# Pooled attention, then a routed mixture of experts: keys pooled by adding DMAs, no padding rows, a bf16 scale, shorter routing pieces at the end of attention

## Chip, cores, metric

The kernel runs on one core of one Trainium2 chip. The metric is the device time of one execution in microseconds (us). Three runs of the kernel before took 1842.59, 1843.52 and 1837.3 us; the median is 1842.59 us. The profiled execution took 1847.69 us, of which the trace spans 1845.2 us.

## The reference

Shapes: four batches, 12288 query rows each (384 x 32), 128 channels; 768 pooled keys per batch; 8 experts with 1024 hidden units.

```
kv_pool = kv.reshape(B, H//4, 4, W//4, 4, C).mean(axis=(2, 4))
k = v   = kv_pool.reshape(B, -1, C) @ w_sr
x       = softmax(q @ k^T / sqrt(C)) @ v          # 49152 rows of 128
active  = (x @ w_skip) > 0                         # about half of the rows
e_idx   = argmax(x @ w_gate);  gate = softmax(x @ w_gate)[e_idx]
out     = x;   out[active] += gate * (relu(x @ w1[e_idx]) @ w2[e_idx])
```

## The kernel before

**Attention.** The 49152 query rows are 384 tiles of 128, 96 per batch. The instructions of every engine are in the order in which the loop over `t` issues them. In round `t` PE computes the scores of tile `t` (L595 to L597), the weighted sum of tile `t - 6` (`attend`, L658) and transposes of tile `t - 1` (L633); DVE takes the row maximum (L603) and low halves in fp16 (L616, L641), ACT the exponential (L608) and high halves (L612, L640), POOL low halves of q (L577). SP transposes probabilities by DMA (L620).

**Keys.** While batch `b` runs, `load_kv` fetches the keys of batch `b + 1`: for each of 6 chunks, four DMAs from SP of 256 KB, one about every 3.25 tiles, each into a part of its own of the tile `kvt`. `pool_kv` then adds 16 values to one on POOL: seven additions of 128x256 (L437) and one of 128x128 (L440) for a chunk, one in a tile. `with_max` lets each wait for the low half L616, so that it runs beside the row maximum. Batch 0 is pooled in another way ahead of the loop. At tile 84 of a batch the projections for the next one begin (`prep_kv`).

**Routing.** Every 12 tiles (a round `r` of 32) `route` finds expert and place of each row and POOL writes the rows, one indirect DMA for a tile (L183 by L792), to a scratch tensor `scr`, where each expert has a region that is filled upward. Per-expert totals are carried from round to round in `run`, by a matmul (L766). Round 31 alone is cut into three pieces of 4 tiles, whose small operations run on DVE (`few`); rounds up to 30 use 12 tiles and POOL.

**Experts.** Groups of 2048 rows are read back from the upper end of each region; a last group reaches below the region's begin, where 2048 padding rows per expert (32 DMAs of 264 KB, `write_pads`) hold a row number that no write accepts. A group is four sub-steps of 512 rows: `up` (24 matmuls), `down` (24 matmuls), and in the next sub-step `finish`: 4 transposes, 4 scaled additions on DVE (L292) and 4 indirect DMAs into the output. `x_transpose` splits a sub-step's rows in fp16 halves (L247, L255) and transposes them by DMA (L258). `w_scale` finds a power of two for each weight matrix; the maximum over partitions is an fp32 matmul with ones (L197).

**Between the two.** The first group is chosen early (`snapshot`, round 27), its rows are loaded by `first_step`, and its steps (`peel`) are interleaved with the end of attention, two in a round from round 384 on. `make_table` lists all other groups; `flush` then loads the next group. A barrier follows, and the loop over 17 groups (L1006).

**Queues.** Each engine runs its instructions in order. SP issues all DMAs but the indirect ones, so a wait in front of one holds all behind it. POOL issues the indirect ones.

Of the kernel before, what the change touches and what calls it, by code (L numbers as in the profile page):

```python
# [20 lines left out]
RT = 12  # L21
# [3 lines left out]
def kernel(  # L25
# [28 lines left out]
    K1, K2 = 3, 2  # L54
# [24 lines left out]
    BIG = 1 << 20  # L79
    NG = -(-NT // G) + E  # L80
# [4 lines left out]
    scr = dram.tile([E * CAP, ROW], F32, name="scr")  # L85
# [43 lines left out]
    e0 = consts.tile([1, E], F32, name="e0")  # L129
# [3 lines left out]
    def iconst(name, shape, pattern, base):  # L133
        ti = consts.tile(shape, I32, name=name + "_i")
        nc.gpsimd.iota(ti, pattern=pattern, base=base, channel_multiplier=0)
        tf = consts.tile(shape, F32, name=name)
        nc.gpsimd.tensor_copy(tf, ti)
        return tf

    kg = iconst("kg", [1, KMAX], [[G, KMAX]], 0)  # L140
    gi = iconst("gi", [1, NG + 1], [[1, NG + 1]], 0)
    lo_i = iconst("lo_i", [1, E, E], [[1, E], [-1, E]], 0)
# [11 lines left out]
    w_dg = wp.tile([P, 2, P], F32, name="w_dg")  # L154
# [6 lines left out]
    h = {}  # L161

    def alloc_h(pool):
        h.update(hi=pool.tile([P, FC, ST], F16, name="h_hi"), lo=pool.tile([P, FC, ST], F16, name="h_lo"))

    op = ctx.enter_context(tc.tile_pool(name="op", bufs=2))
    tb_p = ctx.enter_context(tc.tile_pool(name="tb_p", bufs=1))
    tabi = tb_p.tile([1, 2 * (NG + 1)], I32, name="tabi")
    cumi = tb_p.tile([1, 1], I32, name="cumi")

    writes, first_writes, finished, ready, loaded, moved = [], [], [], [], [], []
# [19 lines left out]
    def w_scale():  # L191
        for i, w in enumerate((w1_raw, w2_raw.rearrange("p k c -> p (k c)"))):
            nc.vector.tensor_reduce(out=w_max[:, i:i + 1], in_=w, axis=AX.X, op=ALU.max, apply_absolute_value=True)
            nc.vector.tensor_scalar(out=w_dg[:, i, :], in0=ident, scalar1=w_max[:, i:i + 1], scalar2=None, op0=ALU.mult)
# [4 lines left out]
        nc.vector.tensor_scalar(out=w_max, in0=w_max, scalar1=2.0 ** -80, scalar2=None, op0=ALU.max)  # L199
        em = emask.broadcast_to([P, 2])  # L200
        nc.vector.tensor_tensor(out=w_exp[:, 2:4], in0=w_max.bitcast(I32), in1=em, op=ALU.bitwise_and)
        nc.vector.tensor_tensor(out=w_exp[:, 0:2], in0=w_exp[:, 2:4], in1=em, op=ALU.bitwise_xor)
        wf = w_exp.bitcast(F32)
        for i, p in enumerate((WEXP - 1, W2EXP - 1)):
            nc.vector.tensor_scalar(out=w_sc[:, i:i + 1], in0=wf[:, i:i + 1], scalar1=2.0 ** p, scalar2=None,
                                    op0=ALU.mult)
# [29 lines left out]
    def load_start(gidx):  # L236
        return nc.sync.value_load(tabi[0:1, bass.ds(gidx + (NG + 1), 1)], min_val=0, max_val=E * CAP - G)

# [6 lines left out]
    def x_transpose(s, pool=False):  # L245
        for t in range(TT):
            nc.scalar.activation(out=x16[:, 0, t, :], in_=xin[s][:, t, 0:C], func=AF.Copy,  # L247
                                 scale=xin[s][:, t, C + 2:C + 3])
        if pool:
# [3 lines left out]
            nc.gpsimd.tensor_tensor(out=x16[:, 1, :, :], in0=x, in1=x16[:, 0, :, :], op=ALU.subtract)  # L253
        for t in () if pool else range(TT):
            nc.vector.scalar_tensor_tensor(out=x16[:, 1, t, :], in0=xin[s][:, t, 0:C],  # L255
                                           scalar=xin[s][:, t, C + 2:C + 3], in1=x16[:, 0, t, :],
                                           op0=ALU.mult, op1=ALU.subtract)
        nc.sync.dma_start_transpose(xT[s], x16.rearrange("p a t c -> p (a t c)"))  # L258
# [27 lines left out]
    def finish(s):  # L286
        ps = alloc["x"]()
        for t in range(TT):
            nc.tensor.transpose(ps[:, t * P:(t + 1) * P], yTs[s % 2][:, t * P:(t + 1) * P], ident)  # L289
        o = op.tile([P, TT, C], F32, name="o")  # L290
# [4 lines left out]
        for t in range(TT):  # L295
            scatter_rows(out, xin[s].bitcast(I32)[:, t, C + 1:C + 2], o[:, t, :], NT - 1, "out")

    def make_table():
        en = ends[0:1, :]
        cnt = tb_p.tile([1, E], F32, name="cnt")  # L300
        nc.vector.tensor_tensor(out=cnt, in0=en, in1=base0[0:1, :], op=ALU.subtract)
        cmp = tb_p.tile([1, E, KMAX], F32, name="cmp")
        nc.vector.tensor_tensor(out=cmp, in0=cnt.unsqueeze(2).broadcast_to([1, E, KMAX]),
                                in1=kg.unsqueeze(1).broadcast_to([1, E, KMAX]), op=ALU.is_gt)
        yield
        ng = tb_p.tile([1, E], F32, name="ng")
        nc.vector.tensor_reduce(out=ng, in_=cmp, axis=AX.X, op=ALU.add)
        nc.vector.tensor_tensor(out=ng, in0=ng, in1=e0, op=ALU.subtract)
        nc.vector.tensor_tensor(out=lo_i, in0=lo_i, in1=ng.unsqueeze(1).broadcast_to([1, E, E]), op=ALU.mult)
        cum = tb_p.tile([1, E], F32, name="cum")  # L310
        nc.vector.tensor_reduce(out=cum, in_=lo_i, axis=AX.X, op=ALU.add)
        nc.vector.tensor_scalar(out=cumi, in0=cum[:, E - 1:E], scalar1=1.0, scalar2=None, op0=ALU.max)
        yield
        av = tb_p.tile([1, E], F32, name="av")
# [4 lines left out]
        S3 = [1, NG + 1, E]  # L319
        ge = tb_p.tile([1, NG + 1, E + 1], F32, name="ge")  # L320
# [3 lines left out]
        tab = tb_p.tile([1, 2, NG + 1], F32, name="tab")  # L324
        nc.vector.tensor_reduce(out=tab[:, 0, :], in_=ge[:, :, 1:E + 1], axis=AX.X, op=ALU.add)
        nc.vector.tensor_scalar(out=tab[:, 0, :], in0=tab[:, 0, :], scalar1=float(E - 1), scalar2=None, op0=ALU.min)
        yield
        sel = tb_p.tile(S3, F32, name="sel")
        nc.vector.tensor_tensor(out=sel, in0=ge[:, :, 0:E], in1=ge[:, :, 1:E + 1], op=ALU.subtract)
        nc.vector.tensor_tensor(out=sel, in0=sel, in1=av.unsqueeze(1).broadcast_to(S3), op=ALU.mult)  # L330
        nc.vector.tensor_reduce(out=tab[:, 1, :], in_=sel, axis=AX.X, op=ALU.add)
# [3 lines left out]
        nc.vector.tensor_scalar(out=tab[:, 1, :], in0=tab[:, 1, :], scalar1=0.0, scalar2=None, op0=ALU.max)  # L335
        nc.vector.tensor_copy(tabi, tab.rearrange("p a g -> p (a g)"))

    def peel():
        for s in range(NST):
            for c in range(FC):  # L340
# [10 lines left out]
                if s == NST - 1 and c in (1, 3):  # L351
                    scale = w_scale() if c == 1 else scale
                    next(scale, None)
                yield
            if s == NST - 1:
                split_w1()
            for i, _ in enumerate(down(s)):
                if s == NST - 1 and i == 1:
                    x_transpose(1)
# [5 lines left out]
    with ExitStack() as p1:  # L365
# [25 lines left out]
        PK = 4 if TPB >= 64 else 8  # L391
# [3 lines left out]

        PADS = [(e, i) for e in range(E) for i in range(0, G // P, PK)]

        def write_pads(e, i):
            dst = scr[e * CAP + i * P:e * CAP + (i + PK) * P, :].rearrange("(p k) c -> p k c", p=P)
# [6 lines left out]
        def load_kv(b, k, rs=range(R)):  # L406
# [3 lines left out]
            for r in rs:  # L410
                nc.sync.dma_start(KVT[b, k][:, r, :], src[r])
# [151 lines left out]
        LASTR = NTILE // RT - 1  # L563
        SNAPR = LASTR - 4

# [80 lines left out]
        def attend(t):  # L646
# [23 lines left out]
            def scale():  # L670
# [6 lines left out]
                if r >= LASTR:  # L677
# [8 lines left out]
        def route(r, a, b, last, eng):  # L686
# [41 lines left out]
            if not few:  # L728
                for _ in range(3 if r < LASTR - 1 else K1):
# [9 lines left out]
            for _ in range(1 if few else 2 if r < LASTR - 1 else K2):  # L739
                yield  # L740
            yield (None if r >= LASTR - 1 else GT - 1)
            while accs.get("done", 0) != r * RT + a:
                yield (None if r >= LASTR - 1 else GT - 1)
# [18 lines left out]
            else:  # L762
                wa = E * RTP
                ohf = oha.rearrange("p e t -> p (e t)")
                nc.tensor.matmul(ps[:, 0:wa], ones_bf, ohf, start=True, stop=False)
                nc.tensor.matmul(ps[:, 0:wa].rearrange("p (e t) -> p e t", t=RTP)[:, :, 0], ones_f[0:1, :], run[0:1, :],  # L766
                                 start=False, stop=True)
                nc.tensor.matmul(ps[:, wa:2 * wa], upper_bf, ohf, start=True, stop=True)
                pre = rt.tile([P, E, RTP], F32, name="pre")
                accs["run"] = pre[:, :, RT]  # L770
# [293 lines left out]
```

## Time and profile before

| | us |
|---|---|
| median of three runs | 1842.59 |
| profiled execution | 1847.69 |
| its span in the trace | 1845.2 |
| PE busy in the span | 1757.6 |
| DVE, ACT, POOL busy | 1549.4, 1325.3, 1104.0 |

In 40 slices of 46.13 us, busy share in tenths and granted TensorE clock in tenths, the engines stand so:

```profile
PE   4999999999999999999998879999999999999997
...
DVE  7899889999899898898999768878877888778875
...
POOL 2369887889968998766767543333333333333333
PEclk9999999999999999999999989999999999999998
```

Attention is the first 22 slices, the passage to the experts the next two, the loop the rest. PE is the fullest row nearly everywhere, so the reader looks for slices in which it is not, and for what PE itself could be spared where it is.

### The profile page before, as it was taken

The numbers are of one execution on the slowest core, as the hardware profiler recorded it, in microseconds if no ns is written. First come the engines' busy times: TensorE is split into PE (matmuls) and PEld (weight loads), VectorE is DVE, ScalarE is ACT, GpSimd is POOL, SyncE is SP. The second block draws the span as 40 slices with busy tenths as digits, with TensorE's granted clock in tenths as the row PEclk, the third lists the DMA queues.
The fourth block names the chain that finished last, engine by engine and source line by source line (L and its number), as shares of the span: only waits on it lengthen the run. The fifth ranks groups of instructions, "written<-read, shape, count | busy, mean of one in ns | idle before, by whom it ended". The sixth has DMA issues, their size and how long they took to land. (4 is left out here: it accounts for less than half of the span.)

```text
span 1845.2 us, 42946 instructions
## 1 busy us (share of the span) xinstructions
PE 1757.6 (95%) x14017; PEld 1263.0 (68%) x14017; DVE 1549.4 (84%) x3226; ACT 1325.3 (72%) x2518; POOL 1104.0 (60%) x1339
## 2 busy tenths in 40 slices
PE   4999999999999999999998879999999999999997
PEld 3998889888899888899998434444444444444443
DVE  7899889999899898898999768878877888778875
ACT  2888778888888887788887446666666666666664
POOL 2369887889968998766767543333333333333333
PEclk9999999999999999999999989999999999999998
DMA  6999999999999999999999443333333333333342
GB/s 178 192 202 218 220 185 208 220 184 189 178 177 197 206 214 204 200 215 216 228 211 195 92 119 98 95 99 96 93 95 95 102 93 94 94 97 97 98 112 71
DMA packets 621971, 284.88 MB, mean 154 GB/s; under 512 B 503168, under 2 KB 571904, under 8 KB 621824
## 3 DMA queue, kind: packets, MB, share of 16 engines
q1 hardware_dynamic: 600320, 244.56, 66.1%
q0 software_dynamic: 21504, 38.43, 7.0%
q8 instruction: 83, 1.36, 0.3%
q14 instruction: 64, 0.52, 0.1%
HBM read 90.60 MB, written 78.64 MB: 92 GB/s over the span
## 5 line engine op out<-in xcount | busy, mean ns | idle before, releaser
L183 POOL DMA_INDIRECT out_dram<-o,xin x288 | 294.4, 1022 | 481.9 <-DVE o L292 415.4
L183 POOL DMA_INDIRECT scr<-rows,di x384 | 410.6, 1069 | 120.8 <-issue 98.6
L269 DVE SCALAR_TENSOR_TENSOR h_lo<-h_ps,h_hi 128x512 f16<-128x512 f32 x544 | 343.9, 684 | 145.5 <-ACT h_hi L268 145.5
L608 ACT ACTIVATE p_sb<-s_ps,nm 128x768 f32<-128x768 f32 x384 | 347.4, 905 | 142.7 <-DVE nm L603 140.7
L603 DVE TENSOR_REDUCE nm<-s_ps 128x1 f32<-128x768 f32 x384 | 363.6, 947 | 54.4 <-PE s_ps L597 53.5
L268 ACT ACTIVATE h_hi<-h_ps 128x512 f16<-128x512 f32 x544 | 318.5, 597 | 51.6 <-PE h_ps L267 32.1
L658 PE MATMUL acc_ps<-v_hi,pt 128*128 128x138 f16 x3072 | 321.4, 224 | 16.9 <-DVE rs L666 16.5
L658 PEld LDWEIGHTS <-pt 128*128 128x128 f16 x4608 | 276.8, 98 | 82.7 <-issue 81.8
L616 DVE SCALAR_TENSOR_TENSOR p<-p_sb,p 128x512 f16<-128x512 f32 x384 | 298.1, 776 | 4.2 <-ACT p L612 3.6
L595 PE MATMUL s_ps<-k_hi,q_hi 128*128 128x384 f32 x768 | 294.7, 384 | 0.0
L658 PE MATMUL acc_ps<-v_lo,pt 128*128 128x138 f16 x1536 | 294.4, 223 | 0.0
L596 PE MATMUL s_ps<-k_lo,q_hi 128*128 128x384 f32 x768 | 260.4, 339 | 0.0
L597 PE MATMUL s_ps<-k_hi,q_lo 128*128 128x384 f32 x768 | 259.5, 338 | 0.0
L612 ACT ACTIVATE p<-p_sb 128x512 f16<-128x512 f32 x384 | 243.3, 634 | 11.1 <-DMA pt<-p 8.0
L265 PE MATMUL h_ps<-xT,w_hi 128*128 128x512 f16 x544 | 206.9, 380 | 7.7 <-issue 7.7
L266 PE MATMUL h_ps<-xT,w_hi 128*128 128x512 f16 x544 | 206.9, 380 | 0.0
L267 PE MATMUL h_ps<-xT,w_lo 128*128 128x512 f16 x544 | 206.8, 380 | 0.0
L281 PE MATMUL y_ps<-h_hi,w_hi 128*128 128x512 f16 x544 | 206.2, 379 | 0.0
L281 PE MATMUL y_ps<-h_hi,w_lo 128*128 128x512 f16 x544 | 206.2, 379 | 0.0
L281 PEld LDWEIGHTS <-w_hi 128*128 128x128 f16 x1152 | 112.7, 98 | 132.4 <-issue 0.4
L284 ACT ACTIVATE yT<-y_ps,y_sc 128x512 f32<-128x512 f32 x68 | 46.8, 688 | 216.2 <-PE y_ps L281 216.2
L281 PE MATMUL y_ps<-h_lo,w_hi 128*128 128x512 f16 x544 | 195.1, 379 | 0.0
(216 smaller groups left out, 3208.1 us busy)
## 6 DMA issues: line engine op xcount, KB each, us to landing
kvt<-in_kv_dram SPq DMA_DIRECT2D x96, 256.0 KB
q_sb<-in_q_dram SPq DMA_DIRECT2D x96, 256.0 KB
out_dram<-rows SPq DMA_DIRECT2D x96, 256.0 KB
xin<-scr SPq DMA_DIRECT2D x75, 264.0 KB, 2.9
w_raw<-in_moe_w_dram SPq DMA_DIRECT2D x38, 512.0 KB, 4.3
scr<-pad SPq DMA_DIRECT2D x32, 264.0 KB
pt<-p SPq DMA_TRANSPOSE x384
scr<-rows,di POOLq DMA_INDIRECT x384
```

Of the source, the lines that this page charges most:

```text
L183: ins = nc.gpsimd.indirect_dma_start(out=dst, out_offset=bass.IndirectOffsetOnAxis(ap=ids, axis=0), in_=src, in_offset=None, bounds_check= ...
L268: nc.scalar.activation(out=h["hi"][:, c, :], in_=ps, func=AF.Relu)
L269: nc.vector.scalar_tensor_tensor(out=h["lo"][:, c, :], in0=ps, scalar=0.0, in1=h["hi"][:, c, :], op0=ALU.max, op1=ALU.subtract)
L281: nc.tensor.matmul(ps, w[:, c, :], h[x][:, c, :], start=(i == 0), stop=(i == len(terms) - 1))
L595: nc.tensor.matmul(s[:, h, :HK], q_hi, k_hi[:, sl], start=True, stop=False)
L596: nc.tensor.matmul(s[:, h, :HK], q_hi, k_lo[:, sl], start=False, stop=False)
L597: nc.tensor.matmul(s[:, h, :HK], q_lo, k_hi[:, sl], start=False, stop=True)
L603: nc.vector.tensor_reduce(out=NM[t], in_=S_PS[t][:, :, :HK], axis=AX.XY, op=ALU.max, negate=True)
L608: nc.scalar.activation(out=P_SB[t], in_=S_PS.pop(t)[:, :, :HK], func=AF.Exp, bias=NM.pop(t))
L612: nc.scalar.activation(out=P16[t][:, 0, :], in_=p_flat(t)[:, 0:KD * P], func=AF.Copy, scale=2.0 ** PEXP)
L616: LO[:] = [nc.vector.scalar_tensor_tensor(out=p16[:, 1, :], in0=p_flat(t)[:, 0:KD * P], scalar=2.0 ** PEXP, in1=p16[:, 0, :], op0=ALU.mult ...
L658: nc.tensor.matmul(ps[:, j % 2, :], w, v[a][:, k, :], start=(i == 0), stop=(i == len(AVL) - 1))
```

## The change

Keys of batches 1 to 3: SP loads the first of four parts; three DMAs from POOL add the others to it in place. One addition of 128x256 and the last of 128x128 stay on POOL. Padding rows of the experts go; one dummy region of 2048 rows at the end of `scr` stays (4 DMAs). Instead `make_table` works out how far a group reaches below its region (`low`), and `finish` writes row numbers into a tile of its own (`own`), raised where a row lies below. `w_scale` cuts the row maxima to powers of two first and multiplies in bf16. Rounds 30 and 31 are routed in pieces of 4 tiles. Loads of the first group wait only for scatters up to round 27. In the last batch, totals are added on POOL instead of by L766. `x_transpose` has two buffers; output writes of the first group are held back behind the last scatters (`held`); the next group's first two loads come ahead of the transposes of its rows; from round 390 on one step of the first group goes in a round.

```
 def load_kv(b, k, rs=range(R)):
     for r in rs:
-        nc.sync.dma_start(KVT[b, k][:, r, :], src[r])
+        if b == 0 or r == 0:
+            nc.sync.dma_start(KVT[b, k][:, r, :], src[r])
+        else:
+            nc.gpsimd.dma_start(KVT[b, k][:, 0, :], src[r], accum_op=ALU.add)
 def pool_kv(b, k):
-    n = R * R * C
+    n = R * R * C if b == 0 else R * C
-PADS = [(e, i) for e in range(E) for i in range(0, G // P, PK)]
+PADS = list(range(0, G // P, PK))
 def w_scale():
+    nc.vector.tensor_tensor(out=w_max.bitcast(I32), in0=w_max.bitcast(I32), in1=emask..., op=ALU.bitwise_and)
-    nc.tensor.matmul(ps[:, 0:2 * P], ones_f, w_dg.rearrange("p a x -> p (a x)"), start=True, stop=True)
+    nc.tensor.matmul(ps[:, 0:2 * P], ones_bf, w_dg.rearrange("p a x -> p (a x)"), start=True, stop=True)
 def finish(s, g=None):
+    nc.vector.scalar_tensor_tensor(out=own, in0=place[:, s, :].unsqueeze(2), scalar=low[:, bass.ds(g, 1)],
+                                   in1=ids, op0=ALU.add, op1=ALU.max)
+    if g is None and not ready: held.append(write)
+    else: write()
 def peel():
-    if s == NST - 1 and c in (1, 3): ... next(scale, None)
-    if s == NST - 1: split_w1()
+    if s == NST - 1 and c == 6: x_transpose(1)
+    scale = w_scale() if s == NST - 1 else ()          # first half behind the last up
     for i, _ in enumerate(down(s)):
-        if s == NST - 1 and i == 1: x_transpose(1)
+        if s == NST - 1 and i == 1: next(scale, None); split_w1()
-                if r >= LASTR:
+                if r >= FEWR:                          # LASTR - 1
 def route(...):
+    totals = r * RT < NTILE - TPB
+    if not totals: eng.tensor_tensor(out=accs["run"], in0=run, in1=pre[:, :, RT], op=ALU.add)
+                   eng.tensor_tensor(out=acc, in0=acc, in1=em(run), op=ALU.add)
 def load_rows(st, s, after, group=None):
+    tc.declare_no_dep(ins, group="scr", keep=after, reason="rows read first are complete")
-            while finished and (finished[0] == 0 or len(moved) > 1):
+            while finished and (finished[0] <= 1 or len(moved) > 1):
-            for _ in range(2 * (t >= NTILE)): next(first)
+            for _ in range(0 if t < NTILE else 2 if t < NTILE + LAG else 1): next(first)
```

On POOL, while batch 0 runs, a stretch of the order before (`q_lo` is the low half of q, `kvt` the key tile, `pooled` its sum, `oh_all` a routing tile):

```order
L437 TENSOR_TENSOR kvt<-kvt 128x256
L183 DMA scr<-rows,di 409600x132
L437 TENSOR_TENSOR kvt<-kvt 128x256
L183 DMA scr<-rows,di 409600x132
L577 TENSOR_TENSOR q_lo<-q_sb,q_hi 128x256
L437 TENSOR_TENSOR kvt<-kvt 128x256
L183 DMA scr<-rows,di 409600x132
L440 TENSOR_TENSOR pooled<-kvt 128x128
```

and the same place now:

```order
L188 DMA scr<-rows,di 411648x132
L443 DMA kvt<-in_kv_dram 128x1x512
L188 DMA scr<-rows,di 411648x132
L610 TENSOR_TENSOR q_lo<-q_sb,q_hi 128x256
L188 DMA scr<-rows,di 411648x132 x2
L771 TENSOR_TENSOR oh_all_94<-oh,act 128x12x8
L610 TENSOR_TENSOR q_lo<-q_sb,q_hi 128x256
L443 DMA kvt<-in_kv_dram 128x1x512
```

Additions on POOL have become DMAs that POOL issues, in among the scatters.

On POOL from the scatters of round 29 to the barrier in front of the loop, before (`di` are places, `xin` rows read back, `o` results):

```order
L789 IOTA rows 128x12
L183 DMA scr<-rows,di 409600x132 x12
L789 IOTA rows 128x4
L183 DMA scr<-rows,di 409600x132 x4
L789 IOTA rows 128x4
L183 DMA scr<-rows,di 409600x132 x4
L183 DMA out_dram<-o,xin_134 49152x128 x4
L789 IOTA rows 128x4
L183 DMA scr<-rows,di 409600x132 x4
L183 DMA out_dram<-o,xin_135 49152x128 x4
L183 DMA out_dram<-o,xin_136 49152x128 x4
L993 TENSOR_LOAD cumi
```

and now:

```order
L827 IOTA rows 128x12
L188 DMA scr<-rows,di 411648x132 x2
L827 IOTA rows 128x4
L188 DMA scr<-rows,di 411648x132 x6
L827 IOTA rows 128x4
L188 DMA scr<-rows,di 411648x132 x12
L827 IOTA rows 128x4
L188 DMA scr<-rows,di 411648x132 x4
L827 IOTA rows 128x4
L188 DMA scr<-rows,di 411648x132 x4
L827 IOTA rows 128x4
```

The first piece before begins with round 30 (round 29 stands ahead of it); now round 29's twelve stand in among the first two pieces of round 30, four pieces follow (the last two have the same two rows again), and all twelve output writes come after the last scatter.

On SP, the loads of the next group (`xin_134` is the first 512 rows, `xT_142` and `xT_139` are the transposed rows of the first group's last sub-step and of the next group's first), before:

```order
L258 DMA_TRANSPOSE xT_142<-x_138 128x8x128
L224 TENSOR_LOAD tabi
L224 ISA x2
L231 ISA
L231 DMA w_raw<-in_moe_w_dram 128x1024
L234 ISA
L234 DMA w_raw<-in_moe_w_dram 128x8x128
L237 TENSOR_LOAD tabi
L237 ISA x2
L189 ISA
L189 DMA xin_134<-scr 128x528
L258 DMA_TRANSPOSE xT_139<-x_138 128x8x128
```

and now (`xin_139`, `xT_147`, `xT_144` are the same three):

```order
L240 DMA w_raw<-in_moe_w_dram 128x8x128
L243 TENSOR_LOAD tabi
L243 ISA x2
L194 ISA
L194 DMA xin_139<-scr 128x528
L264 DMA_TRANSPOSE xT_147<-x16b 128x8x128
L194 ISA
L194 DMA xin_140<-scr 128x528
L264 DMA_TRANSPOSE xT_144<-x_143 128x8x128
```

The load, which waits for the last scatter, now stands ahead of the transpose that the first group's last sub-step needs.

## Rows read from the trace of the kernel before

**Rows 1.** Stretch, length; busy PE, PEld, DVE, ACT, POOL (count); PEclk, DMA share, GB/s.

```profile
311.00:492.00 181.00, 175.20 (x1887) 161.21 (x1885) 165.39 (x312) 149.39 (x280) 161.57 (x202) 1.00 1.05 195
804.50:950.00 145.50, 144.46 (x1568) 133.40 (x1565) 130.52 (x268) 123.00 (x233) 99.15 (x131) 1.00 1.12 221
...
1100.00:1800.00 700.00, 700.00 (x3372) 336.65 (x3371) 557.62 (x1250) 451.53 (x866) 263.71 (x258) 1.00 0.37 97
```

**Rows 2.** The row maximum, once a tile: stretches of batches 0, 1, 2, 3.

```profile
L603 DVE TENSOR_REDUCE nm<-s_ps x72: 887/950/959, 64.6 to 244.2; 128x1 f32<-128x768 f32 x72
...
L603 DVE TENSOR_REDUCE nm<-s_ps x72: 889/950/958, 311.1 to 490.3; 128x1 f32<-128x768 f32 x72
...
L603 DVE TENSOR_REDUCE nm<-s_ps x61: 893/950/959, 557.3 to 710.6; 128x1 f32<-128x768 f32 x61
...
L603 DVE TENSOR_REDUCE nm<-s_ps x60: 893/950/959, 804.7 to 949.0; 128x1 f32<-128x768 f32 x60
```

**Rows 3.** Groups with shapes, batch 1 (311 to 492 us).

```profile
L183 POOL DMA_INDIRECT scr<-rows,di x71 | 77.8, 1096 | 15.2 <-issue 11.5 <-POOL rows L789 2.5 <-DVE nm L603 0.5
...
L616 DVE SCALAR_TENSOR_TENSOR p<-p_sb,p 128x512 f16<-128x512 f32 x72 | 57.3, 796 | 0.7 <-ACT p L612 0.7
...
L437 POOL TENSOR_TENSOR kvt<-kvt 128x256 f32<-128x256 f32 x38 | 32.9, 865 | 0.5
```

**Rows 4.** The same groups, batch 3 (804.5 to 950 us).

```profile
L183 POOL DMA_INDIRECT scr<-rows,di x59 | 61.9, 1049 | 26.7 <-issue 25.4 <-POOL rows L789 0.7 <-DVE ptq L641 0.3
...
L616 DVE SCALAR_TENSOR_TENSOR p<-p_sb,p 128x512 f16<-128x512 f32 x60 | 43.7, 728 | 2.1 <-ACT p L612 2.1
```

**Rows 5.** PE, timeline, in the loop: start us, us, instruction.

```profile
1160.83 0.59 PE L197 MATMUL x_ps<-w_dg,ones_f 128*128 128x256 f32 x2
1161.26 0.38 PE L281 MATMUL y_ps<-h_hi,w_hi 128*128 128x512 f16 x1
1161.48 0.38 PE L281 MATMUL y_ps<-h_hi,w_lo 128*128 128x512 f16 x1
```

**Rows 6.** PE, timeline, end of attention; in brackets the idle before.

```profile
1012.02 0.29 PE L658 MATMUL acc_ps<-v_hi,pt 128*128 128x138 f16 x2
...
1013.11 0.38 PE L633 MATMUL acc_ps<-ident,p_sb 128*128 128x128 f32 x2
...
1019.53 0.38 PE L766 MATMUL misc<-pre,ones_f 1*128 1x8 f32 x2
1019.85 0.22 PE L768 MATMUL misc<-oh_all,upper_bf 128*128 128x104 bf16 x1
...
1026.15 0.19 PE L754 MATMUL misc<-oh_few,upper_bf 128*128 128x40 bf16 x1 [3.70 <-DVE acc L775]
...
1070.43 0.67 PE L197 MATMUL misc<-w_dg,ones_f 128*128 128x256 f32 x2 [3.10 <-DVE w_dg L194]
...
1088.22 0.58 PE L265 MATMUL h_ps<-xT,w_hi 128*128 128x512 f16 x1 [7.67 <-issue]
```

**Rows 7.** POOL, timeline, the same stretch.

```profile
1003.64 1.09 POOL L183 DMA_INDIRECT scr<-rows,di  x1 [1.60 <-issue]
...
1034.63 1.05 POOL L183 DMA_INDIRECT scr<-rows,di  x1 [7.84 <-DVE di L788]
1035.99 0.98 POOL L183 DMA_INDIRECT scr<-rows,di  x1 [0.30 <-issue]
...
1080.26 1.08 POOL L183 DMA_INDIRECT out_dram<-o,xin  x1 [0.30 <-issue]
```

**Rows 8.** SP's DMA queue, timeline, the same stretch.

```profile
1072.54 0.35 SPq L189 DMA_DIRECT2D xin<-scr  x1
...
1083.67 1.24 SPq L258 DMA_TRANSPOSE xT<-x  x1
```

**Rows 9.** DMA issues: count, KB each, median us to landing.

```profile
xin<-scr SPq DMA_DIRECT2D x75, 264.0 KB, 2.9
...
xT<-x SPq DMA_TRANSPOSE x74, 3.5
```

More of the change, by code (lines that the diff above doesn't have):

```diff
@@ L79 @@
     BIG = 1 << 20
+    LOWER = 1 << 19
+    assert NT <= LOWER and NT // P * P == NT
     NG = -(-NT // G) + E
@@ L168 @@
     tabi = tb_p.tile([1, 2 * (NG + 1)], I32, name="tabi")
+    low = tb_p.tile([P, NG + 2], F32, name="low")
     cumi = tb_p.tile([1, 1], I32, name="cumi")
-    writes, first_writes, finished, ready, loaded, moved = [], [], [], [], [], []
+    writes, first_writes, finished, ready, loaded, moved, held = [], [], [], [], [], [], []
     sync_dep = mybir.DependencyInfo(mybir.DependencyClass.Sync, mybir.DependencyReason.DATA)
@@ L289, in finish @@
             nc.tensor.transpose(ps[:, t * P:(t + 1) * P], yTs[s % 2][:, t * P:(t + 1) * P], ident)
+        ids = xin[s].bitcast(I32)[:, :, C + 1:C + 2]
+        own = op.tile([P, TT, 1], I32, name="ids")
+        if g is None:
+            nc.vector.tensor_copy(own, ids)
+        else:
+            nc.vector.scalar_tensor_tensor(out=own, in0=place[:, s, :].unsqueeze(2), scalar=low[:, bass.ds(g, 1)], in1=ids,
+                                           op0=ALU.add, op1=ALU.max)
         o = op.tile([P, TT, C], F32, name="o")
@@ L563 @@
         LASTR = NTILE // RT - 1
+        FEWR = LASTR - 1
         SNAPR = LASTR - 4
@@ L776, in route @@
                 eng.tensor_scalar(out=gs, in0=gs, scalar1=1e-9, scalar2=x_sc, op0=ALU.add, op1=ALU.mult)
+                if not totals:
+                    eng.tensor_tensor(out=accs["run"], in0=run, in1=pre[:, :, RT], op=ALU.add)
+                    eng.tensor_tensor(out=acc, in0=acc, in1=em(run), op=ALU.add)
             accs["done"] = r * RT + b
@@ L798, in snapshot @@
             if run is None:
-                for x in (e0, snap, snap_i):
-                    nc.vector.memset(x, 0.0)
+                nc.vector.memset(e0, 0.0)
+                nc.vector.memset(snap_i[:, 0:1], 0)
+                nc.vector.memset(snap_i[:, 1:2], E * CAP)
                 return
-            cs = small.tile([1, E], F32, name="cs")
-            nc.vector.tensor_tensor(out=cs, in0=run[0:1, :], in1=base0[0:1, :], op=ALU.subtract)
-            most = small.tile([1, 1], F32, name="most")
+            cs = small.tile([P, E], F32, name="cs")
@@ L805, in snapshot @@
+            nc.vector.tensor_tensor(out=cs, in0=run, in1=base0, op=ALU.subtract)
+            most = small.tile([P, 1], F32, name="most")
             nc.vector.tensor_reduce(out=most, in_=cs, axis=AX.X, op=ALU.max)
-            nc.vector.scalar_tensor_tensor(out=cs, in0=cs, scalar=most, in1=em8[0:1, :], op0=ALU.is_equal, op1=ALU.mult)
-            first = small.tile([1, 1], F32, name="first")
+            nc.vector.scalar_tensor_tensor(out=cs, in0=cs, scalar=most, in1=em8, op0=ALU.is_equal, op1=ALU.mult)
@@ L813, in snapshot @@
-            nc.vector.scalar_tensor_tensor(out=snap[:, 1:2], in0=most, scalar=float(G), in1=snap[:, 1:2],
-                                           op0=ALU.mult, op1=ALU.add)
+            nc.vector.tensor_scalar(out=e0, in0=em8, scalar1=first, scalar2=most, op0=ALU.is_equal, op1=ALU.mult)
+            nc.vector.tensor_scalar(out=snap[:, 0:1], in0=first[0:1], scalar1=float(E), scalar2=None, op0=ALU.add)
+            at = small.tile([1, 1], F32, name="at")
+            nc.vector.tensor_scalar(out=at, in0=first[0:1], scalar1=float(CAP), scalar2=float(G), op0=ALU.mult,
+                                    op1=ALU.add)
@@ L815, in snapshot @@
+            nc.vector.tensor_scalar(out=snap[:, 1:2], in0=at, scalar1=most[0:1], scalar2=float(E * CAP), op0=ALU.mult,
+                                    op1=ALU.add)
             nc.vector.tensor_copy(snap_i, snap)
@@ L843, in flush @@
         def flush():
-            if not ready or not moved:
+            if not ready:
                 return
@@ L984 @@
                         pools.append(pool_kv(b + 1, k))
-            for _ in range(2 * (t >= NTILE)):
+            for _ in range(0 if t < NTILE else 2 if t < NTILE + LAG else 1):
                 next(first)
-        for _ in make_table():
-            next(first)
+        for i, _ in enumerate(make_table()):
+            if i % 2:
+                next(first)
         ready.append(True)
+        flush()
+        for write in held:
+            write()
         flush()
```

151 lines of the change are left out of this document (82 added, 69 removed).

## The prediction

> **What bounds the kernel now.** I read the busy row of PE over 40 slices first: it is full in attention and in the loop, and thin only where one passes into the other. The busy time by stretch [rows 1] says how full. In the loop PE is busy 700.00 of 700 us, so there only work taken from PE itself counts. In batch 3, in which no keys are pooled, it is busy 144.46 of 145.5; in batch 1 only 175.20 of 181. POOL is the engine that differs, with 161.57 of 181 against 99.15 of 145.5. The row maximum comes once a tile, so its first and last start give the pace [rows 2]: (244.2 - 64.6)/71 = 2.530 us a tile in batch 0, 2.524 in batch 1, 2.555 in batch 2 and 2.446 in batch 3. Batches 0 to 2, which pool keys, pay 0.084, 0.078 and 0.109 us a tile. The groups by shape show where: the fp16 low half on DVE, beside which POOL adds, takes 796 ns in batch 1 and 728 in batch 3, and a scatter's issue 1096 ns and 1049 [rows 3, 4]. The end of attention is read last, engine by engine [rows 6 to 8]: each of PE and POOL waits there for small operations on DVE, and the loop begins at 1088.22.
>
> **Keys.** Of six chunks in each of three batches, six of seven wide additions go: 108 x 0.865 = 93.4 us of POOL [rows 3]. In come 54 DMAs that POOL issues. No row shows an adding DMA; the nearest is the scatter, 1.096 and 0.30 us of issue around it [rows 3, 7], so 54 x 1.4 = 75.4 us. POOL is thus little emptier, but what goes is what runs beside DVE's two-operand work. The most that this can give is the whole excess over batch 3, for 84 tiles in each: 84 x (0.084 + 0.078 + 0.109) = 22.8 us. From PE's idle time it is (5.80/72 - 1.04/60) = 0.063 us a tile [rows 1, 2], times 252 = 15.9. I take 14, near the second and a little under it, because the new issues also stand on POOL among scatters and low halves that PE's order waits for. The other end is a loss, which the third rival prices.
>
> The Trainium skill (SBUF — State Buffer, section "SBUF: two separate sides") says that VectorE with two inputs in SBUF and a GpSimd operation that reads SBUF lock each other out for a whole instruction. The rows show a part of it, 68 ns on the mean of the low half and not 865. By it the term would be 252 x 0.068 = 17 us instead of 14, if each nanosecond of DVE were passed on.
>
> **Padding rows.** 28 writes of SP go. They lie in batch 3, where PE is idle 1.04 us in all of the stretch [rows 1]; bounds 0 and -1, value 0. The own row numbers that replace them cost four small DVE operations a sub-step in the loop, where DVE is busy 557.62 of 700 us beside a full PE [rows 1]: nothing, and the full cost only if DVE were the later one.
>
> **Totals.** In the last batch the fp32 matmul of one row goes from six rounds; it holds PE from 1019.53 to 1019.85 [rows 6], 6 x 0.32 = 1.9 us, of a PE that is full. The POOL addition that replaces it stands behind nothing that PE needs at once.
>
> **bf16 scale.** In the loop the fp32 pair holds PE from 1160.83 to 1161.26, 0.43 us, and a 512-column fp16 matmul 0.22 [rows 5]. One 256-column bf16 matmul for each of the two halves is not in the rows; by columns, half of 0.22 for one pass, 0.11, and 0.22 if a short one pays as much as a long one. Over 17 groups the saving is 17 x 0.32 = 5.5 us, with bounds 3.6 and 7.3 (the whole pair). I take 5.5, since the pair itself shows time that goes by columns. PE is never idle there, so it is all gained. The added mask on DVE is one operation a matrix and lies behind `up`.
>
> **The tail.** The term is how much sooner the loop begins than 1088.22. Two chains end in front of its barrier.
>
> PE first. Last scores are out at 1012.02 and an `attend` takes 1.09 us from there to 1013.11 [rows 6]. The three pieces added in round 30 are DVE work: one piece holds PE 3.70 us at 1026.15 [rows 6]; three in rounds that have other work to do I estimate at 3 us in all. Then 1012.0 + 3 + 7 x 1.09 + 48 x 0.2155 (a 512-column matmul [rows 5]) + 1 for small routing matmuls = 1034 at the end of the first sub-step, and three sub-steps more of 48 x 0.2155 + 0.44 for transposes: 1066.3. Between the third and the fourth there is a new wait: SP issues the next group's first load, which waits for the last scatter, ahead of the transpose of the last sub-step's rows, and behind SP's wait stand also that transpose and so PE's last `up`. With the scatters ending at about 1056 (below) and 3.5 us from a transpose's issue to landing [rows 9], against an `up` due at 1055.5, this costs 3 to 4; I take 3. The scale's wait of 3.10 us [rows 6] now has half of its work in front of `down`; I take 1.4. PE ends at 1070.7.
>
> POOL second. Before, round 30's first scatter waits 7.84 us for its places on DVE and starts at 1034.63 [rows 7]; the pieces now come while round 29's rows still go out, so I let POOL run through. From 1003.64 + 3, 48 slots (36 scatters, 12 held writes) of 0.98 + 0.30 us [rows 7] are 61.6, and row numbers for seven pieces some 3: 1071.2, and 3 of waits for results that PE has just made: 1074. The scatters alone are out at 1056. Now POOL's last write starts at 1080.26 [rows 7].
>
> POOL is the later. From the last transpose's end, 1083.67 + 1.24 [rows 8], to the first matmul at 1088.22 are 3.3 us, so the loop begins near 1077, 11 us earlier. Bounds: with no DVE delay and no wait, 1003.64 + 64.6 + 3.3 = 1071.5, -17; with PE's waits of 3.70 and 3.10 us [rows 6] merely moved to other places, -11 + 6.8 = -4.
>
> **The sum** is made against the profiled execution, 1847.69 us: -14 - 1.9 - 11 - 5.5 = -32.4, so 1815.3. That execution is 5.1 us above the median of 1842.59, which it is taken from alike: 1810.
>
> **Rivals.** First, key pooling pays nothing: what POOL loses in additions it gets back in issues (93.4 against 75.4 us), and scatters stay as long as they are. For it: POOL's share hardly falls. Against: batch 3 has as many scatters and runs at 2.446. Then -18.4: 1824.
>
> Second, the tail gains nothing. One wait of SP, for the last scatter, holds two loads and two transposes; if the pieces' places come late on DVE, the last scatter ends near 1067 and not 1056, `up` waits with it and the twelve held writes come behind. For it: the load is issued only at 1072.54 now, and POOL has waited 7.84 us for DVE [rows 7, 8]. Against: all other routing stands earlier in the order. Then -21.4: 1821.
>
> Third, slower: an adding DMA holds POOL. In batch 1 POOL is idle 19.43 us in 72 tiles [rows 1, 2], 0.27 a tile; a chunk's 13 tiles have 3.5 us, and six additions gone give 5.2, so 8.7 us for three issues, or 2.9 for one. Up to 2.9 us an issue is hidden; beyond it each microsecond costs 54. With the other terms at -18.4 the kernel is slower than before from 2.9 + 18.4/54 = 3.3 us. At 4 us: 54 x 1.1 - 18.4 = +41, 1883. For it: no row shows what such an issue costs, and the scatter's 1.1 us is for 128 rows alone. Against: scatters run among full DVE work and grow by 47 ns only.
>
> The Trainium skill (SBUF — State Buffer, section "A bandwidth-pool intuition that's wrong") speaks for it: a DMA that GpSimd issues takes about 620 ns alone and 3100 beside a VectorE copy that holds the shared port. By 3.1 and 0.30 us an issue it would be 54 x 0.5 = 27 us of loss instead of 14 of gain, and the kernel at 1851. Scatters at 1096 ns against 0.98 in the quiet tail [rows 3, 7] show that stretch only as a tenth.
>
> **Chances.** The forecast, with keys, tail and loop all paying something (1795 to 1820): 0.62. Keys pay nothing 0.17; tail pays nothing 0.12; both nothing and the loop's gain lost besides, within 0.3% of before, 0.04; slower by an adding DMA that holds POOL 0.05. A measurement of this kernel can't tell less than 0.3%, 5.5 us, from no change. Range: best case with every upper bound 22.8 + 1 + 1.9 + 17 + 7.3 = 50, which I cut at 48, so 1795; on the other side one rival and a half, -9: 1834. Faster 0.91, same 0.04, slower 0.05.
>
> **What would show it.** Keys: the pace of batches 0 to 2 near 2.47 us a tile, the low half near 740 ns, POOL's issue line for keys about 1.1 us each; an issue above 2.9 us with PE idle behind POOL makes the forecast wrong. Loop: the scale's matmuls near 0.11 us start to start, and the loop shorter by 5 to 6 us. Tail: scatters back to back from about 1007 on the old clock, a wait of PE for a transpose ahead of the last `up`, and the loop starting 8 to 14 us after what the pace has already given. If the loop starts as long after the last scores as now, 76 us, the tail step failed.

## The result and the profile after

The changed kernel takes 1826.52 us (median of seven runs, 1822.31 to 1831.99) against 1842.59: a ratio of 0.9918, with a 95% interval of 0.9897 to 0.9938. That is 16.1 us faster, where 32.4 was forecast. The profiled execution took 1828.98 us, its span 1827.1, 18.1 us less than the span before.

Where the 18.1 us lie is read from the starts of the row maximum, as in [rows 2]. First the whole stretch in which keys are pooled, tiles 6 to 276, then tiles 360 to 383, in which rounds 30 and 31 are routed, for the kernel before:

```profile
L603 DVE TENSOR_REDUCE nm<-s_ps x271: 887/950/959, 49.8 to 740.6; 128x1 f32<-128x768 f32 x136
...
L603 DVE TENSOR_REDUCE nm<-s_ps x24: 892/948/958, 952.0 to 1012.8; 128x1 f32<-128x768 f32 x24
```

and for the changed one, where the line is L636:

```profile
L636 DVE TENSOR_REDUCE nm<-s_ps x271: 886/950/959, 49.0 to 734.1; 128x1 f32<-128x768 f32 x136
...
L636 DVE TENSOR_REDUCE nm<-s_ps x24: 887/950/958, 942.6 to 1012.3; 128x1 f32<-128x768 f32 x24
```

Pooling's 270 tiles went from 690.8 to 685.1 us. Up to tile 360 the kernel is 9.4 us ahead. The tiles behind it, beside which the added pieces are routed, then take 69.7 us instead of 60.8, which gives 8.9 of these back: 3.7 up to tile 372 and 5.2 from there (33.9 us instead of 28.7). From the last maximum to the loop it is 8.2 us quicker. So from tile 360 to the loop, 136.2 us (952.0 to 1088.22) became 136.9 (942.6 to 1079.51): the end of attention as a whole gained nothing. Counted from tile 372 alone it is 104.1 and 101.1 us. From the loop's first matmul to PE's last it is 739.3 us instead of 748.4.

The busy times by stretch, which answer to [rows 1] (columns as there), of batch 1, batch 3 and the loop:

```profile
305.00:486.00 181.00, 176.82 (x1892) 162.90 (x1890) 162.60 (x312) 149.66 (x282) 152.41 (x188) 0.99 1.15 197
...
798.00:944.00 146.00, 145.35 (x1589) 135.31 (x1587) 133.47 (x273) 126.09 (x237) 105.41 (x143) 1.00 1.06 194
...
1100.00:1800.00 700.00, 700.00 (x3381) 334.75 (x3380) 569.64 (x1327) 453.18 (x870) 250.19 (x258) 1.00 0.37 97
```

POOL is emptier in batch 1 by 9 us of 181, PE is fuller by 1.6, and the DMA engines' share has risen from 1.05 to 1.15. The loop is still all PE. In it the scale's matmul, before [rows 5], now is one, and the next starts 0.11 us later:

```profile
1238.29 0.27 PE L205 MATMUL x_ps<-w_dg,ones_bf 128*128 128x256 bf16 x1
1238.40 0.38 PE L287 MATMUL y_ps<-h_hi,w_hi 128*128 128x512 f16 x1
```

From one group's scale matmul to the next it is 43.30 us in all groups, before 43.62. The end of attention on PE, which answers to [rows 6]:

```profile
992.65 0.19 PE L787 MATMUL misc<-oh_few,upper_bf 128*128 128x40 bf16 x1 [3.01 <-DVE acc L810]
...
1045.80 0.38 PE L287 MATMUL acc_ps<-h_lo,w_hi 128*128 128x512 f16 x1 [1.63 <-DVE h_lo L275]
...
1059.46 0.38 PE L271 MATMUL up_ps<-xT,w_hi 128*128 128x512 f16 x1 [1.92 <-DMA xT<-x16b]
...
1072.18 0.39 PE L205 MATMUL misc<-w_dg,ones_bf 128*128 128x256 bf16 x1 [4.36 <-DVE w_dg L202]
...
1079.51 0.38 PE L271 MATMUL h_ps<-xT,w_hi 128*128 128x512 f16 x1 [2.18 <-issue]
```

and on POOL and SP, which answer to [rows 7, 8]: the first and last scatter, the last write, and SP's load ahead of the transpose for which PE waits at 1059.46.

```profile
1001.73 1.10 POOL L188 DMA_INDIRECT scr<-rows,di  x1 [4.62 <-issue]
...
1049.21 0.97 POOL L188 DMA_INDIRECT scr<-rows,di  x1 [0.30 <-issue]
...
1068.00 1.14 POOL L188 DMA_INDIRECT out_dram<-o,ids  x1 [0.30 <-DVE x16b L261]
```

```profile
1055.00 0.35 SPq L194 DMA_DIRECT2D xin<-scr  x1
1055.45 1.29 SPq L264 DMA_TRANSPOSE xT<-x16b  x1
```

Scatters run back to back and end 21 us sooner (the last one ended at 1070.98 before); but the loop waits for PE, not for POOL, as `tail2` shows below.

Kernels timed together ran on one chip, beside the kernel before, which took 1843 us there in the second set below and 1884 to 1892 in the others. In those others every trace has some 20 to 45 us more between tile 340 and the loop, much of it in waits that the trace ends with "issue" or "remote"; so ratios to the kernel before are compared, and the tail is read from the second set alone.

### The profile page after: what moved, and what is told of

Same layout as the page of the kernel before. It is cut to its first block, busy times and chain, and to the rows that moved or that the text cites. A ratio compares the mean times of both kernels' runs of the same rounds, so it can differ in the third digit from the quotient of the medians.

```text
span 1827.1 us, 42624 instructions
## 1 busy us (share of the span) xinstructions
PE 1747.9 (96%) x13997; PEld 1256.9 (69%) x13997; DVE 1547.6 (85%) x3344; ACT 1325.0 (73%) x2522; POOL 1049.8 (57%) x1294
## 5 line engine op out<-in xcount | busy, mean ns | idle before, releaser
L188 POOL DMA_INDIRECT out_dram<-o,ids x288 | 280.0, 972 | 494.1 <-DVE o L306 427.6
L636 DVE TENSOR_REDUCE nm<-s_ps 128x1 f32<-128x768 f32 x384 | 363.8, 947 | 53.7 <-PE s_ps L630 50.7
L649 DVE SCALAR_TENSOR_TENSOR p<-p_sb,p 128x512 f16<-128x512 f32 x384 | 288.7, 752 | 17.3 <-ACT p L645 16.1
```

Source lines behind the costliest of these rows:

```text
L188: ins = nc.gpsimd.indirect_dma_start(out=dst, out_offset=bass.IndirectOffsetOnAxis(ap=ids, axis=0), in_=src, in_offset=None, bounds_check= ...
L636: nc.vector.tensor_reduce(out=NM[t], in_=S_PS[t][:, :, :HK], axis=AX.XY, op=ALU.max, negate=True)
L649: LO[:] = [nc.vector.scalar_tensor_tensor(out=p16[:, 1, :], in0=p_flat(t)[:, 0:KD * P], scalar=2.0 ** PEXP, in1=p16[:, 0, :], op0=ALU.mult ...
```

## Experiments

**First set: keys alone, pooling left out, pieces left out.** `keys_only` is the kernel before with the first two hunks of the change (`load_kv`, `pool_kv`). `no_pool` and `no_load` are the kernel before with

```
-            n = R * R * C
+            n = R * R * C if b == 0 else R * C
```

and in `no_load` parts `r > 0` of batches 1 to 3 aren't loaded either. `few31` is the changed kernel with

```
-        FEWR = LASTR - 1
+        FEWR = LASTR
```

> The kernel before with the key loading and pooling of the change alone: three adding DMAs a chunk, two additions left. Theory 1 (the prediction's: POOL's additions beside DVE are what batches 0 to 2 pay over batch 3): 14 us faster than before, ratio 0.992, tiles 6 to 372 shorter by 14. Theory 2 (the stretch of batch 3 that I compared with was the quickest part of that batch, and the additions cost little): 4 to 6 us faster, 0.997. Theory 3 (additions cost 14 or more, but adding DMAs cost nearly as much in their place): 4 to 6 us faster too; the next two kernels tell 2 from 3.

> The kernel before, in which six of seven wide additions a chunk are left out for batches 1 to 3 (the keys are then the sum of one part in four); the 72 loads from SP stay. No adding DMAs. Theories 1 and 3: 14 to 23 us faster than before. Theory 2: at most 9 us faster, as the whole of batch 3 (78 tiles in 194.1 us) says against 196.8, 196.2 and 197.9 in the others.

> As the last, and the loads of three of four parts are left out as well for batches 1 to 3: neither additions nor adding DMAs nor their bytes. Against the kernel with adding DMAs alone this prices the 54 adding DMAs: theory 1 and 2 within 3 us of it, theory 3 some 10 us faster than it.

> The changed kernel with one number put back: only round 31, not 30, is routed in pieces of 4 tiles on DVE. In the profile of the changed kernel tiles 372 to 383 take 33.9 us against 28.7 before, and from tile 372 to the loop 101.1 against 104.1. If the added pieces on DVE are what took the tail's gain (theory A): tiles 372 to 383 near 29 again, but scatters of round 30 late by some 8 us; the kernel 0 to 5 us faster than the changed one. If the pieces pay more than they cost (theory B), as the end of scatters at 1050 against 1071 says: 5 to 10 us slower than the changed one.

`keys_only`: 1889.45 against 1891.97 us, ratio 0.9982 (0.9961 to 1.0002): 0 to 7 us on 1843, not 14. Keys left out change the routing and so the number of groups, so the next two (1661.39 and 1667.85 us in all) are read by their tiles 6 to 276. Without additions they take 678.9 us, without loads as well 682.1, 11.9 and 8.7 less than before, while those of `keys_only` take 690.6, no less than before. As far as single profiles tell, that is nearest to its theory 3. Without additions:

```profile
L603 DVE TENSOR_REDUCE nm<-s_ps x271: 889/951/959, 49.4 to 728.3; 128x1 f32<-128x768 f32 x136
```

The low half says why. In the kernel before, from 60 to 730 us, and then without additions (mean ns after the busy time):

```profile
L616 DVE SCALAR_TENSOR_TENSOR p<-p_sb,p 128x512 f16<-128x512 f32 x262 | 205.2, 783 | 1.2 <-ACT p L612 0.7 <-ACT p_sb L608 0.5
```

```profile
L616 DVE SCALAR_TENSOR_TENSOR p<-p_sb,p 128x512 f16<-128x512 f32 x267 | 191.0, 715 | 1.4 <-ACT p L612 0.8 <-issue 0.3 <-ACT p_sb L608 0.3
```

So the mechanism of the prediction exists, 68 ns an operation, but the 11.9 and 8.7 us that come of leaving the additions out are about half, or less, of the 22.8 that I had set as the most. With three adding DMAs the low half takes 743 to 760 ns in nine traces (760 in the changed kernel), although only 17 or 18 wide additions are left in this stretch, as many as in `no_pool`. So with the adding DMAs 23 to 40 of the 68 ns are won, not all. `few31` took 1881.66 us, 0.9949 (0.9923 to 0.9975); its tail is among the lengthened ones, so it was run again.

**Second set: the changed kernel, old keys, pieces, two moves.** `old_keys` is the changed kernel with both key hunks taken back. `tail2` moves two things in the changed kernel:

```
+            if s == NST - 2: scale = w_scale(); next(scale)      # ahead of down(s)
+                if s == NST - 1 and c == 1: next(scale, None)    # in up
-            scale = w_scale() if s == NST - 1 else (); next(iter(scale), None)
-                if s == NST - 1 and i == 1: next(scale, None); split_w1()
+                if s == NST - 1 and i == 1: split_w1()
-            while finished and (finished[0] <= 1 or len(moved) > 1):
+            while finished and moved and (finished[0] <= 1 or len(moved) > 1):
```

> The changed kernel once more, as the anchor for the next three on the same chip: 0.992 of the kernel before if that ratio holds on another chip; its tiles 6 to 276 again near 685 us against 691 before, tiles 372 to 383 near 34, the loop near 739.

> The changed kernel with the old key loading and pooling (all additions on POOL, no adding DMA), all else as changed. If the keys' part is worth 14 us (the prediction) it is 14 us slower than the changed kernel; if additions cost about 10 and adding DMAs 5 to 6 in their place (what the two kernels without additions say: 11.9 and 8.7 us over tiles 6 to 276), 3 to 6 us slower, all of it before tile 276.

> The changed kernel with pieces of 4 tiles in round 31 alone. Theory A (the pieces of round 30 on DVE ate the tail's gain): tiles 372 to 383 near 29 instead of 34 us, and the kernel as fast as the changed one or up to 5 us faster. Theory B (they pay): tiles 372 to 383 shorter all the same, but scatters end some 8 us later, SP's load and the last transpose with them, and the kernel is 3 to 8 us slower.

> The changed kernel with two steps of the first group moved: the maxima of the next weights are taken ahead of the third `down` and their matmul goes behind the second `up` part of the last sub-step (in the changed kernel PE waits 4.36 us for them, followed by 6.83 us at half clock); and SP's load of the next group comes behind the transpose of the last sub-step's rows, for which PE waits 1.92 us. If these two waits set the loop's start (the chain on PE, not POOL's writes, which end 8 us ahead of it), the loop begins 4 to 9 us earlier. If POOL's writes or the barrier set it, at most 1 us.

The changed kernel: 1829.76 us against 1843.46, 0.9924 (0.9901 to 0.9946). With the old keys: 1828.66 us, 0.9925 (0.9902 to 0.9947). On this chip the keys paid nothing; its tiles 6 to 276 took 686.3 us, those of the changed kernel 686.2. A single profile settles such a number badly: `few31_again`, which is the same kernel up to tile 360, took 694.3. Over all sets these tiles take 684 to 695 us in nine traces with three adding DMAs (mean 688.4) and 686 to 696 in four with the old keys (mean 691.1).

`few31_again`: 1837.12 us, 0.9959 (0.9946 to 0.9972), 7.4 us slower than the changed kernel. Theory B holds. Its tiles 360 to 383 are back at 60.9 us (953.1 to 1014.0), but two rows on PE show what the late scatters then do:

```profile
1075.87 0.59 PE L271 MATMUL up_ps<-xT,w_hi 128*128 128x512 f16 x1 [10.93 <-DMA xT<-x16b]
...
1091.13 0.28 PE L205 MATMUL misc<-w_dg,ones_bf 128*128 128x256 bf16 x1 [3.98 <-DVE w_dg L202]
```

```profile
1071.56 0.35 SPq L194 DMA_DIRECT2D xin<-scr  x1
1072.01 1.33 SPq L264 DMA_TRANSPOSE xT<-x16b  x1
```

SP's load waits for the last scatter until 1071.56, the transpose stands behind it, and PE waits 10.93 us for that: the second rival's mechanism, which the pieces keep small in the changed kernel (1.92). From tile 360 to the loop it is 144.8 us, 136.9 and 136.8 in two profiles of the changed kernel. So the pieces, which cost 7.5 to 8.9 us ahead of the last scores, pay 8 on balance, and the other edits of the tail without them are 8.6 slower than the kernel before (136.2). This is one profile, of the slowest of ten executions; by the times the pieces pay 7.4.

`tail2`: 1820.70 us, 0.9877 (0.9857 to 0.9896), 9.1 us faster than the changed kernel; tile 360 to the loop in 128.5 us (942.6 to 1071.10). Two of PE's waits behind the last scores:

```profile
1056.90 0.38 PE L271 MATMUL up_ps<-xT,w_hi 128*128 128x512 f16 x1 [0.73 <-DMA xT<-x16b]
...
1071.10 0.59 PE L271 MATMUL h_ps<-xT,w_hi 128*128 128x512 f16 x1 [3.01 <-issue]
```

The wait for the scale is gone, and with it the half clock. In the changed kernel the granted clock was 0.50, the 1.2 GHz level, right where PE stands and starts again, at 1072.18, behind that wait:

```profile
1070.00:1076.80 6.80, 4.62 (x12) 1.79 (x13) 4.43 (x12) 1.15 (x1) 0.00 (x0) 0.50 0.28 55
```

In `tail2` no half clock is granted between 1056 and 1068 us. So the PE chain set the loop's start.

**Third set: each move alone, the bf16 maximum alone, two adding DMAs.**

> The changed kernel with the first of the two moves alone that made the tail 7 to 8 us shorter: maxima of the next weights ahead of the third `down`, their matmul behind the second part of the last `up`. If PE's wait of 4.3 us and the half clock behind it are most of what went, 0.989 of the kernel before: 5 to 7 us of the two moves' 9, and the wait for the last transpose stays at 2. If they only give way to a later wait, under 3 us.

> The changed kernel with the second move alone: SP's load of the next group behind the transpose of the last sub-step's rows. PE's wait for that transpose falls from 1.9 to under 1 us; the wait of 4.3 us for the scale stays, since the scale's operations on DVE follow the last `up`. 1 to 2 us faster than the changed kernel, if moves add up.

> The kernel before with the bf16 maximum alone. The loop's groups 43.30 us instead of 43.62 (17 x 0.32 = 5.5 us, as the prediction has it), and 0.997 of the kernel before. PE's wait of 4.09 us at the loop's exit, which all kernels with the old code show and none with the new (0.78): gone, if the number of matmuls in the loop sets it, and then 3.3 us more, 0.995; there still, if it comes with the other edits.

> The changed kernel with both moves of the tail, and with two adding DMAs a chunk instead of three, each into a part of its own (SP loads two parts; three wide additions instead of one), so that no adding DMA waits for the one before it: POOL waited 20.6 us at the 54 for a transfer. If that wait is what adding DMAs cost (5 to 6 us over tiles 6 to 276), 3 to 5 us faster than with both moves alone (0.9877). If additions cost as much as they do, none.

`scale_early` 1864.97 us, 0.9881 (0.9836 to 0.9926), and `xt_first` 1866.62, 0.9890 (0.9852 to 0.9928): too wide to part 5 us from 2, and the changed kernel didn't run in this set. In the traces each takes its own wait: none for the scale and 1.0 us for the transpose in the one, 4.4 for the scale and none for the transpose in the other.

`bf16_only`, the kernel before with the hunk in `w_scale` alone: 1878.67 us, 0.9964 (0.9944 to 0.9985), 6.6 us on 1843. Its groups take 43.30 us. The wait at the loop's exit is not touched by it:

```profile
1870.44 1.09 PE L290 MATMUL x_ps<-ident,yT 128*128 128x128 f32 x4 [4.08 <-PEq L1007]
```

`two_adds` (with both moves) has SP load two parts and adds each of the others into one of them; three wide additions a chunk stay on POOL:

```
-                if b == 0 or r == 0:
+                if b == 0 or r < 2:
                     nc.sync.dma_start(KVT[b, k][:, r, :], src[r])
                 else:
-                    nc.gpsimd.dma_start(KVT[b, k][:, 0, :], src[r], accum_op=ALU.add)
+                    nc.gpsimd.dma_start(KVT[b, k][:, r - 2, :], src[r], accum_op=ALU.add)
```

1856.10 us, 0.9859 (0.9824 to 0.9894); POOL no longer waits at an adding DMA.

**Fourth set: zero, two, three and six adding DMAs a chunk, all with both moves.** What was open is by what adding DMAs cost about as much as the additions in their place: by POOL's wait from one to the next, by their issues on POOL, or by their bytes. `t2_split` cuts each of three into two of half the width:

```
-                    nc.gpsimd.dma_start(KVT[b, k][:, 0, :], src[r], accum_op=ALU.add)
+                    for x in (0, 2 * C):
+                        nc.gpsimd.dma_start(KVT[b, k][:, 0, x:x + 2 * C], src[r][:, :, x:x + 2 * C], accum_op=ALU.add)
```

> The changed kernel with both moves of the tail, as anchor for the next three (54 adding DMAs, one wide addition a chunk): 0.988 of the kernel before.

> The same with the old key pooling (no adding DMA, seven wide additions a chunk). If the adding DMAs pay as the prediction had it, 14 us slower than the anchor. If an adding DMA costs POOL and its neighbours what two additions do (0 us between the changed kernel and it with the old keys so far), within 4 us of it.

> The same with 36 adding DMAs, each into a part of its own, and three wide additions a chunk. If the waits of POOL between adding DMAs into one part (20.6 us in 15 of 54) are what eats the gain: 3 to 5 us faster than the anchor. Otherwise within 3 us of it.

> The same as the anchor with each adding DMA cut into two of half the width: 108 issues with the same bytes. If it is the issue on POOL that costs (54 more at 1.0 us and more, 75 us, on an engine that has some 0.27 us a tile of idle time and got 93 back): 5 to 10 us slower than the anchor. If it is the bytes or the adding in the DMA engines, within 3 us.

| adding DMAs a chunk | us | ratio to before (95%) |
|---|---|---|
| 0 (`t2_old`) | 1872.29 | 0.9902 (0.9885 to 0.9920) |
| 2 (`t2_two`) | 1863.40 | 0.9860 (0.9837 to 0.9882) |
| 3 (`t2_three`) | 1867.17 | 0.9882 (0.9862 to 0.9902) |
| 6 of half width (`t2_split`) | 1886.41 | 0.9975 (0.9955 to 0.9995) |

Three pay 0.0020, 3.7 us on 1843, and the intervals overlap; two pay 7.7, clear of them. Two are 4 us faster than three, as they would be if POOL's waits counted, but there the intervals overlap. Cutting them adds 54 issues and 0.0093, 17 us: 0.32 us each, though POOL is not full. In the changed kernel and in `t2_split`, 60 to 730 us:

```profile
L443 POOL DMA_DIRECT2D kvt<-in_kv_dram x51 | 50.0, 980 | 20.9 <-DMA kvt<-in_kv_dram 20.6 <-issue 0.2
```

```profile
L447 POOL DMA_DIRECT2D kvt<-in_kv_dram x98 | 91.5, 1096 | 10.9 <-DMA kvt<-in_kv_dram 9.8 <-issue 1.0
```

The cut also halves the runs of bytes, so issue and run length aren't told apart.

**Fifth set: more buffers behind the transposes.** ACT's waits over 60 to 730 us show what is new with adding DMAs. The kernel before, then the changed one (us in total, times, longest):

```profile
ACT p_sb L608 <- DVE nm L603: 94.8, 158, 3.0
...
ACT p L612 <- DMA pt<-p: 2.0, 5, 1.0
```

```profile
ACT p_sb L641 <- DVE nm L636: 62.7, 136, 1.3
ACT p L645 <- DMA pt<-p: 30.2, 34, 2.3
```

What ACT no longer waits for DVE, it waits for a DMA transpose to have read its buffer: 96.8 us in all before, 92.9 after. It is 2.0, 3.1 and 2.1 us in three kernels with additions alone (before, `old_keys`, `t2_old`), 20 to 38 in nine traces with 54 adding DMAs, and 12.2 in `t2_split`, the slowest with 108, so this wait alone doesn't set the time. The transposes themselves stand longer on SP's queue. The kernel before, then the changed one (ns: least, median, most):

```profile
L620 SPq DMA_TRANSPOSE pt<-p x262: 1231/1277/3798, 60.0 to 728.3; - x131
```

```profile
L653 SPq DMA_TRANSPOSE pt<-p x265: 1231/1414/5292, 59.5 to 729.3; - x133
```

The last two kernels are `t2_three` and `t2_two` with six of these buffers:

```
-        hl = p1.enter_context(tc.tile_pool(name="hl", bufs=4))
+        hl = p1.enter_context(tc.tile_pool(name="hl", bufs=6))
```

> The changed kernel with both moves of the tail and six buffers instead of four for the fp16 probabilities that the DMA transposes read. With adding DMAs ACT waits some 24 to 32 us over 60 to 730 us for a transpose to have read its buffer, without them 2 to 3. If that wait is where the keys' gain went, it falls under 10 us and the kernel is 4 to 8 us faster than with four buffers (0.988 of the kernel before). If the late transposes then hold PE (which needs them six tiles later), or the wait was not on the path, within 3 us of it.

> The same with two adding DMAs a chunk, each into a part of its own (0.986 of the kernel before with four buffers): by the same reason 0.982 to 0.984, otherwise 0.986. The better of the two is the version that I would keep.

1862.14 us, 0.9866 (0.9835 to 0.9898), and 1863.15 us, 0.9863 (0.9840 to 0.9887). ACT's wait is 0.4 us in the first; PE's own for the transposes rose from 1.4 to 7.3:

```profile
PE acc_ps L694 <- DMA pt<-p: 7.3, 8, 2.3
...
ACT p L648 <- DMA pt<-p: 0.4, 1, 0.4
```

With three adding DMAs 0.0016 faster, with two none: within the intervals. Two more buffers take ACT's wait away, move a part of it to PE, and gain nothing that can be told from noise. So it is not shown that the late transposes are what took the keys' gain.

## Why the prediction was half right

**Keys: −14 forecast, 0 to −4 measured (0.9982, 0.9925 against 0.9924, 0.9882 against 0.9902).** This is one of the two steps that failed. Its first half was right: additions on POOL slow the low half, and without them 783 ns become 715. Its second half, that the issues cost only their place on POOL, was wrong. Additions left out give 8.7 to 11.9 us, adding DMAs in their place 0 to 4, so the DMAs cost some 5 to 12 themselves: the low half comes down to 743 to 760 only, transposes stand longer on SP's queue, and 54 issues more (with every adding DMA cut in two) cost 0.32 us each while POOL still has idle time. Which of these sets the price stays open. The bound was too wide as well: batch 3's pace of 2.446 was taken from 60 quick tiles [rows 2]; 78 tiles of it took 194.1 us, 2.49 each, which makes the excess over 84 tiles of each other batch about 9 us and not 22.8.

**The first rival** had the keys' outcome right, though not its reason: POOL did grow emptier, by 9 us of 181. That its 1824 us lie near the measured time is luck: it kept 11 us for the tail, which paid nothing, and had no term for the loop's exit, which gave 3.3.

**The third rival.** An adding DMA holds POOL 0.98 us and not 3.3, so it fell. The 3100 ns that the Trainium skill (SBUF — State Buffer, section "A bandwidth-pool intuition that's wrong") has for a DMA beside a VectorE copy are the time of the DMA; the prediction put them in as POOL's time at its issue. No run here tests that figure: none of DVE's large operations in this stretch is such a copy, and the 51 issues above took 980 ns beside them.

**Totals and bf16: right.** Round 28 (tiles 336 to 347, by the row maximum), without L766, took 28.63 us against 29.07 (0.32 forecast, and 0.36 and 0.37 in rounds 27 and 29). The loop's groups are shorter by 0.32 us, 17 times, as forecast, so the new row numbers cost nothing there, as forecast too.

**The tail: −11 forecast, +0.7 and +0.6 measured from tile 360 (two profiles against one of the kernel before).** This is the other step that failed. POOL's chain came out as worked: from its first scatter, 1001.73 instead of the assumed 1006.6, it ended at 1069.1, 67 us later as forecast. What failed is "PE ends at 1070.7" and so "POOL is the later". First, the pieces cost PE 8.9 us ahead of the last scores (7.5 in the second profile), where I had 3; counted from the last scores, as my sign with 76 us does, this is not seen. Second, the estimated chain from last scores to PE's end, without these 3, was 55.7 us, and it took 66.1 (1011.25 to 1077.3). The step "I take 1.4" for the scale was 4.36, since between the maxima and the matmul stand only twelve matmuls of `down`, 2.6 us; behind that wait 4.6 us of PE's work ran at 0.50, which cost about 2.3; three waits for DVE (1.25, 1.85, 1.63) were not in the sum. `tail2` takes the wait and this half clock away, with 1.2 of the 1.92 for the transpose, and gives 9 us. The second rival, that the tail gains nothing, had the size right and not the mechanism: the last scatter began at 1049.21, not near 1067. `few31_again` shows its mechanism, and against it the pieces are worth 7.4 us by the times and 8 by the profiles.

**Not foreseen:** PE's last transposes wait at the loop's exit, 4.09 us in the kernel before and 0.78 now.

```profile
1835.76 0.90 PE L289 MATMUL x_ps<-ident,yT 128*128 128x128 f32 x4 [4.09 <-PEq L1006]
```

```profile
1818.16 0.66 PE L295 MATMUL x_ps<-ident,yT 128*128 128x128 f32 x4 [0.78 <-ACT yT L290]
```

The wait is 4.1 us in all five traces with the old code behind the loop and at most 1.3 in those with the new; `bf16_only` excludes the matmul count. Which edit does it stays open. The parts make the span's 18.1 us: 5.7 in tiles 6 to 276 (within what profiles of one kernel differ by), 3.7 more ahead of tile 360 (some 2 of them totals), −0.7 in the tail, 5.5 in the loop, 3.3 at its exit, and 0.6 in smaller pieces.

Two sums of the prediction are off in the last digit, without weight: 48 x 1.28 is 61.4 and not 61.6, and 2.9 + 18.4/54 is 3.2 and not 3.3.

The best version that ran is the changed kernel with both moves and two adding DMAs a chunk: 0.9860 (0.9837 to 0.9882) and 0.9859 in two sets.

## What to carry to other kernels

Before counting a contention as gain, leave the whole contender out on the chip: what that gives is the ceiling, and what the replacement itself costs comes off it, which only a run with the replacement alone shows. Start a tail's clock ahead of the first thing that was moved, or its cost is booked elsewhere. In a tail of chained small waits sum the chain of every engine with its present waits, and ask for each moved step how much work stands between it and the one that needs it. A load that waits for the last of something belongs behind every transfer on its queue that doesn't.

## What the hardware showed

An adding DMA's issue holds POOL 0.98 us, and 1.10 at half the width: as long as a scatter's (1.05 to 1.10). DMA transposes of probabilities stand longer on SP's queue while adding DMAs run: 1.41 us in the median instead of 1.28, and ACT's wait for them grew from 2 to 30 us over 670.
